# Two more split units per batch, paced indexed stores and moved small copies in a Fourier-mixing and maxout kernel

## The chip, the cores and the metric

The kernel runs on one core of one Trainium2 chip. The core has a matrix engine (TensorE, PE in the profile; its weight loads are PEld), a vector engine (VectorE, DVE), a scalar engine (ScalarE, ACT), a general engine (GpSimd, POOL) and a queue engine for transfers (SyncE, SP). Each engine works through its own instructions strictly in the order in which they were written; between engines, semaphores order the work. SBUF is the on-chip memory of 128 partitions, PSUM the accumulator memory into which PE writes, in banks of 512 float32 values for each partition. The metric is device time in microseconds (us) for one execution.

## The reference

```python
def _attn_ref(x):                      # x: (8, 3072, 256)
    X = np.fft.fft(x, axis=1)
    X = np.fft.fft(X, axis=2)
    return X.real.astype(np.float32)

def _moe_ref(x, w1, w2, w3, w_out):    # x: (24576, 256); w: (256, 768); w_out: (768, 256)
    h = np.maximum(np.maximum(x @ w1, x @ w2), x @ w3)
    return (h @ w_out).astype(np.float32)
```

The output of the first goes into the second as 24576 rows of 256. Inputs and output are float32.

## The kernel before

The Fourier transform over the 256 features is linear, so its cosine and sine matrices are multiplied into the weights once (`product`, `g_all`). The transform over the 3072 positions is done for each of the 8 batches in two steps (class `Mix`): `s` multiplies the input by a small table, `y` and `z` send the result through DRAM to change its layout (batch 0 uses one DVE transpose instead, `t`), and `k` multiplies it by cosine and sine tables into `tE` and `tO`, the parts of a frequency that are even and odd. A frequency and its mirror (3072 minus it) differ in the sign of the odd part alone. So 1536 frequencies are computed, as 3 blocks of 512, and each gives two output rows: "plus" and "minus", or mirror, rows.

The maximum of three products is taken as the maximum of zero and two differences, w2-w1 and w3-w1; the w1 part is added back by a matrix `gw`, which is w1 times the output weights. For one block of 512 frequencies the 768 hidden values come in 6 chunks of 128. One chunk of one block is a **unit**: 18 units a batch, 144 in all, numbered `g`, with `u` the number in its batch. A unit makes `hp` and `hm`, the hidden values of the plus and minus rows. There are two ways:

- A **plain** unit (`unit_plus`, `unit_minus`, `unit_out`) has six PE products of 512 columns: two into each of two banks for plus (L485, L486), then one into each that takes twice the odd part off (L492). ACT applies relu to one bank (L498) and DVE takes the maximum with the other (L499), once for plus, once for minus.
- A **split** unit forms the third difference ahead, in `third`: PE makes the even part e (L841) and the odd part d (L843); ACT copies d times -0.5 into `odd` (L845), DVE adds to e a term of the row that d lacks, the broadcast `vb` times a column of `wcol`, into `even` (L846), and POOL forms even+odd and even-odd (L850 twice). The unit then needs PE for the second difference alone (L860, L861, and L492 for minus), and one DVE operation for each maximum (L862, L874). That is five PE products. `third` is issued two units ahead.

`is_split` decides: from unit 7 on every odd unit; of the even ones, in batches 1 to 7, those in `EXTRA` (0, 4, 8), in batch 7 those in `EXTRA_LAST` (0, 4, 8, 14). When a plain unit follows a split one, the minus part of the old unit is done before the new one begins, otherwise after.

While a block's units run, PE also works off the second layer of the block before, ten steps a unit (`l2_some`, `l2_block`: L565, L572, L549); DVE adds the linear part and moves the results to one of three row buffers (L577). The last block of all goes through `l2_last`. Plus rows are stored by SP (`stores_plus`). Minus rows lie in reversed order, so POOL stores them with indirect DMA (L653): `rows_m` holds a row number for each partition, `stores_minus` lists the stores, and `scatter` takes them from a waiting list, one at u = 8, 10 and 12 and two at u = 14. Each is followed by a tiny memset.

A table `plan` says what else is issued at the end of which unit: the next batch's steps (`ahead`), loads of x for the batch after (`fetch`, a cast DMA from POOL's queue, in two halves of positions times two directions, at units 9, 11, 18 and 19, that is 0 and 1 of the next batch), and the mirrored half of x, copied by ACT (L128, one eighth at each of units 5 to 12, and L137). `u` copies one column of x into `x0u` (POOL, L442 and L443). `v` broadcasts row 0 of tO through DRAM to `vb`.

Before unit 0 of batch 0 there is a head: x arrives in four pieces, DVE and ACT mirror them (L128, L132), PE runs `s` with warm-up products between, DVE computes three tiny columns (`sgn`, `dif`; L217), evicts one result (L403) and transposes (L429), and `k` for block 0 fills `tE` and `tO` (L463). In unit 5 of batch 0 `rows` computes the row numbers on POOL and `column` (L351) the columns of `wcol` with 24 products of one column.

PSUM pools: `ps_f`, three banks, for e, d, the linear part and the steps of `Mix`; `ps_l1`, two, for the second difference of odd units and one bank of plain units; `ps_w3`, one, for the second difference of even split units and the other bank of plain even ones; `ps_o`, two, for the second layer.

Of the kernel before, what the change touches and what calls it, by code (L numbers as in the profile page):

```python
# [27 lines left out]


FIRST_OF = (4, 8, 1)  # L30
EXTRA, EXTRA_LAST = (0, 4, 8), (0, 4, 8, 14)


def _parts(g):

    done = [(12 + i - 1, slice(128 * i + 96, 128 * i + 128)) for i in range(4)]
    for i in range(4 if g < 2 else 3):
        done.append((FIRST_OF[g] + i - 1, slice(128 * i, 128 * i + 96)))
    if g == 2:
        done += [(16, slice(384, 480, 2)), (15, slice(385, 480, 2))]  # L40
    return done
# [3 lines left out]
def kernel(  # L45
# [9 lines left out]
    nc = tc.nc  # L55

    B, S, D = x.shape
# [4 lines left out]
    NHALF = 1536  # L62
# [46 lines left out]
    rows_m = consts.tile([128, 5], INT32, tag="rows_m")  # L109
# [13 lines left out]
    def mirror(b, s0, s1):  # L123

        t = xt[b % 2]
        fn = (nc.vector.tensor_copy, (nc.gpsimd.tensor_copy, nc.vector.tensor_copy)[s0 >= 25],
              nc.scalar.copy)[min(b, 2)]
        fn(out=t[64:128, s0:s1, 1:128], in_=t[0:64, s0:s1, 255:128:-1])  # L128
        if b < 2:
            if b == 0 and s0 < 40:  # L130
                fn = nc.scalar.copy
            fn(out=t[64:128, s0:s1, 0], in_=t[0:64, s0:s1, 128])  # L132

    def mirror_first(b):
# [59 lines left out]
    zero = gen.tile([128, 512], BF16, tag="zero")  # L194
    nc.vector.memset(zero, 0.0)
    nc.vector.memset(x0u, 0.0)
    half_pi = gen.tile([128, 1], FP32, tag="half_pi")
    nc.vector.memset(half_pi, 0.5 * math.pi)
    nc.scalar.activation(out=half_pi, in_=half_pi, func=AX.Sin)
# [145 lines left out]
    def column():  # L345

        psc = ps_f.tile([128, 512], FP32, name="psc", tag="ps")
        for jc in range(NJC):
            for k, (table, wt) in enumerate(((md, w3_bf), (nmd, w1_bf))):
                for fc in range(2):  # L350
                    nc.tensor.matmul(psc[:, jc:jc + 1],  # L351
                                     wt[:, fc * DFF + jc * 128: fc * DFF + jc * 128 + 128],
                                     table[fc][:, 128:129],
                                     start=(k == 0 and fc == 0), stop=(k == 1 and fc == 1))
        nc.scalar.copy(out=wcol, in_=psc[:, 0:NJC])

    def prep_second():
# [25 lines left out]
    class Mix:  # L383
# [55 lines left out]

        def u(self):  # L440
            pair = x0u[:, 32:160].rearrange("p (h z s) -> p h z s", h=2, s=32)[:, :, 0, 0:24]
            nc.gpsimd.tensor_copy(pair, self.x[0:128, 0:48, 0].rearrange("p (s h) -> p h s", h=2))  # L442
            nc.gpsimd.tensor_copy(x0u[:, 56:57], self.x[0:128, 48, 0:1])  # L443

        def x0(self, out):
            psx = ps_f.tile([128, 512], FP32, name="psx", tag="ps")
# [71 lines left out]
    def stores_plus(b, blk, buf, s0=0, s1=4):  # L518

        mine, v = rows_of(b)  # L520
        r, n = FIRST_OF[blk], s1 if blk < 2 else min(s1, 3)
        if s0 < n:
            yield v[0:96, r + s0:r + n, :], buf[0:96, s0:n, :]
        yield v[32 * blk:32 * blk + 32, 12 + s0:12 + s1, :], buf[96:128, s0:s1, :]
        if n < s1:
            yield mine[16:NHALF + 1:16, :], buf[0:96, 3, :]

    def stores_minus(b, blk, buf):

# [119 lines left out]
    def scatter(n):  # L649

        for _ in range(min(n, len(waiting))):
            row, col, p0, p1, src = waiting.pop(0)
            stored(nc.gpsimd.indirect_dma_start(  # L653
                fours, bass.IndirectOffsetOnAxis(ap=rows_m[p0:p1, col:col + 1], axis=0),
                src, None, element_offset=256 * row), "scattered", ("scattered", "direct"))
            nc.gpsimd.memset(mark, 0.0)

# [26 lines left out]
    mirror(0, *FIRST[3])  # L684
    m.s(4, pool=ps_s)
    warm_up(2)
    scal(sgn, pidx, 0.0, ALU.is_equal)
    scal(sgn, sgn, 2.0, ALU.mult, -1.0, ALU.add)
    scal(dif, sgn, 1.0, ALU.subtract)
    m.s(5, pool=ps_s, evict=dve)  # L690
    nc.scalar.activation(out=md_all, in_=vm, func=AX.Sin, scale=float(2.0 * math.pi / 256.0),
                         bias=turn[:, 0:1])
    m.s(6, pool=ps_s)
    m.t()
# [31 lines left out]

    def rows():

        rows_f = gen.tile([128, 5], FP32, tag="rows_f")
        for (c, n, base, cm) in ((0, 2, 766, -8), (2, 1, 767, -8), (3, 1, 252, -8), (4, 1, 764, -4)):  # L730
            iota(rows_f[:, c:c + n], [[-1, n]], base=base, cm=cm)
        adj = gen.tile([128, 2], FP32, tag="adj")
# [23 lines left out]
    def at(b, unit, fn):  # L756
        plan.setdefault((b + unit // UNITS, unit % UNITS), []).append(fn)
# [23 lines left out]
    def fetch(b, k):  # L781
        half, h = divmod(k, 2)
        load_x(b, *HALVES[half], h)
# [96 lines left out]
    for g in range(B * UNITS):  # L880
# [69 lines left out]
```

## Time and profile before

| what | value |
|---|---|
| median of 3 runs | 392.28 us (392.26 to 392.38) |
| profiled execution | 391.42 us, of which the span from first to last instruction is 389.3 |
| granted TensorE clock | 0.998 |
| batch 0, units 0 to 17 | 20 to 69 us |
| batches 1 to 6 | 44.3 us each |
| sums on POOL, L850 | 182 operations, 1271 and 1269 ns each |
| relu on ACT, L498; odd on ACT, L845 | 106 of 600 ns; 91 of 598 ns |
| even on DVE, L846 | 91 of 737 ns |
| hp and hm of split units on DVE, L862 and L874 | 91 of 688 and 91 of 680 ns |
| hp and hm of plain units on DVE, L499 | 106 of 686 to 689 ns |
| indirect stores, L653 | 37 of 997 to 1000 ns |
| x loads issued by POOL, L121 | 36 of 652 ns |

The profile counts an engine as busy while one of its instructions runs. Instructions of one engine overlap in the table: a product on PE is written with its whole way through the array, and a DVE operation with its start-up, so the distance between two starts can be shorter than one duration. A line of the timeline has the start in us, the duration in us, engine, line, operation and tiles; in brackets behind it stands the idle time of the engine before it and what ended that. A line of the stretches has the stretch, its length and the busy time of each engine in it with the number of instructions, then the granted clock, the share of the DMA engines and GB/s.

### The profile page before, as it was taken

Reading aid. Unit: us, or ns where it says so; the run is one execution under the profiler, and the core shown is the slowest. Engines: PE = TensorE matmul, PEld = TensorE weight load, DVE = VectorE, ACT = ScalarE, POOL = GpSimd, SP = SyncE. Lnnn points to the kernel's source line nnn. Section 1 sums busy time; section 2 is a strip of 40 time slices with the busy share of each in tenths; the row PEclk is TensorE's granted clock in tenths of the full one; section 3 lists DMA queues with packets and bytes.
Section 4 is the critical chain, followed back from the end, with each engine's and each line's share of the span. In section 5 each row is a group of like instructions: output and inputs, shape, how many; then the busy total and the mean of one; then the engine's idle time right before and its main releaser. Section 6 shows DMA issues by size and latency. Waiting matters only on the chain.

```text
span 389.3 us, 8092 instructions
## 1 busy us (share of the span) xinstructions
PE 376.2 (97%) x2817; PEld 236.2 (61%) x2817; DVE 327.7 (84%) x552; ACT 248.4 (64%) x453; POOL 314.3 (81%) x363
## 2 busy tenths in 40 slices
PE   6699999999999999999999999999999999999985
PEld 2355566566665666566665666656665666666654
DVE  7788797799797988899797988989887997999972
ACT  6877789567856696567856687567866346434420
POOL 9983576879898898879898898879787887769881
PEclk9999999999999999999999999999999999999999
DMA  7999764585747666475938657575423544212226
GB/s 113 184 183 160 163 145 118 112 168 161 178 141 130 172 176 154 111 128 186 189 120 149 169 151 176 125 128 185 113 94 93 149 138 139 70 31 80 85 89 206
DMA packets 52263, 54.13 MB, mean 139 GB/s; under 512 B 26547, under 2 KB 45009, under 8 KB 51367
## 3 DMA queue, kind: packets, MB, share of 16 engines
q0 software_dynamic: 20272, 26.45, 34.4%
q1 hardware_dynamic: 31418, 26.58, 25.0%
q10 hardware_dynamic: 532, 0.59, 0.5%
q8 instruction: 22, 0.36, 0.3%
q14 instruction: 19, 0.16, 0.1%
HBM read 36.95 MB, written 30.81 MB: 174 GB/s over the span
## 4 chain that ended last, share of the span: by engine, by line
PE 87%; POOL 4%; DVE 4%; DMA 2%; ACT 1%; issue 1%; DVEq 0%; POOLq 0%
PE po L549 30%; PE pse L492 10%; PE pse L860 5%; PE pse L485 5%; PE pse L486 5%; PE d L843 5%; PE e L841 5%; PE pse L861 5%; PE po L572 5%; PE ps L461 3%; PE ps L396 3%; PE pl L565 2%; DMA xt<-in_x_dram 2%; POOL xt L121 1%; POOL plus L850 1%
## 5 line engine op out<-in xcount | busy, mean ns | idle before, releaser
L850 POOL TENSOR_TENSOR plus<-even,odd 128x512 bf16<-128x512 f32 x91 | 115.7, 1271 | 55.4 <-DVE even L846 44.1
L850 POOL TENSOR_TENSOR minus<-even,odd 128x512 bf16<-128x512 f32 x91 | 115.5, 1269 | 0.0
L845 ACT ACTIVATE odd<-d 128x512 f32<-128x512 f32 x91 | 54.4, 598 | 55.8 <-PE d L843 41.9
L862 DVE SCALAR_TENSOR_TENSOR hp<-pse,plus 128x512 bf16<-128x512 f32 x91 | 62.6, 688 | 32.2 <-PE pse L861 27.9
L549 PE MATMUL po<-wout_bf,hp 128*128 128x256 bf16 x576 | 86.1, 273 | 0.0
L498 ACT ACTIVATE stmp<-pse 128x512 bf16<-128x512 f32 x106 | 63.2, 600 | 24.2 <-PE pse L486 11.2
L549 PE MATMUL po<-wout_bf,hm 128*128 128x256 bf16 x576 | 78.6, 273 | 0.0
L549 PEld LDWEIGHTS <-hp 128*128 128x128 bf16 x576 | 56.3, 98 | 26.2
L492 PE MATMUL pse<-tO,gd_all 128*128 128x512 bf16 x197 | 66.1, 380 | 1.3 <-DVE hp L862 1.3
L846 DVE SCALAR_TENSOR_TENSOR even<-vb,wcol,e 128x512 f32<-128x512 bf16 x91 | 67.1, 737 | 0.0
L549 PEld LDWEIGHTS <-hm 128*128 128x128 bf16 x576 | 56.3, 98 | 16.4
L874 DVE SCALAR_TENSOR_TENSOR hm<-pse,minus 128x512 bf16<-128x512 f32 x91 | 61.9, 680 | 0.4
L499 DVE TENSOR_TENSOR hp<-pse,stmp 128x512 bf16<-128x512 f32 x53 | 36.4, 686 | 8.8 <-ACT stmp L498 4.2
L499 DVE TENSOR_TENSOR hm<-pse,stmp 128x512 bf16<-128x512 f32 x53 | 36.5, 689 | 6.7 <-ACT stmp L498 4.3
L485 PE MATMUL pse<-tE,g_all 128*128 128x512 bf16 x106 | 40.2, 379 | 0.8 <-DVE tE L463 0.4
L577 DVE TENSOR_TENSOR kq<-po,even 128x512 f32<-128x512 f32 x60 | 40.9, 682 | 0.0
L128 ACT COPY xt<-xt 64x762 bf16<-64x762 bf16 (+1 forms) x48 | 39.8, 838 | 1.0
L486 PE MATMUL pse<-tO,g_all 128*128 128x512 bf16 x106 | 40.2, 379 | 0.0
L572 PE MATMUL po<-gw,tO 128*128 128x512 bf16 x92 | 34.9, 379 | 0.0
L860 PE MATMUL pse<-tE,g_all 128*128 128x512 bf16 x91 | 34.6, 380 | 0.1
L653 POOL DMA_INDIRECT out_dram<-kq,rows_m x29 | 29.0, 1000 | 6.8 <-issue 5.7
L841 PE MATMUL e<-tE,g_all 128*128 128x512 bf16 x91 | 34.5, 379 | 0.0
(173 smaller groups left out, 511.7 us busy)
## 6 DMA issues: line engine op xcount, KB each, us to landing
xt<-in_x_dram POOLq DMA_DIRECT2D x14, 384.0 KB
db<-tb SPq DMA_DIRECT2D x21, 192.0 KB
out_dram<-obuf SPq DMA_DIRECT2D x8, 384.0 KB
out_dram<-kq SPq DMA_DIRECT2D x8, 384.0 KB
vb<-vd SPq DMA_DIRECT2D x23, 128.0 KB
xt<-in_x_dram POOLq DMA_DIRECT2D x7, 400.0 KB
xt<-in_x_dram POOLq DMA_DIRECT2D x7, 368.0 KB
out_dram<-kq SPq DMA_DIRECT2D x7, 288.0 KB
```

The source lines that it names most:

```text
L485: nc.tensor.matmul(pse[:, 0:n], g_all[:, jc, 2 * i, :], te, start=True, stop=False)
L486: nc.tensor.matmul(pse[:, 0:n], g_all[:, jc, 2 * i + 1, :], to, start=False, stop=True)
L492: nc.tensor.matmul(pse, gd_all[:, jc, i, :], to, start=False, stop=True, skip_group_check=True)
L498: nc.scalar.activation(out=stmp[:, 0:n], in_=pses[0][:, 0:n], func=AX.Relu)
L499: nc.vector.tensor_tensor(out=dst, in0=src3, in1=stmp[:, 0:n], op=ALU.max)
L549: nc.tensor.matmul(po, hcols(jc), wout_bf[:, jc * 256:(jc + 1) * 256], start=False, stop=(jc == NJC - 1), skip_group_check=True)
L572: nc.tensor.matmul(po, to[:, cp], gw[:, 256:768], start=True, stop=True)
L845: nc.scalar.activation(out=odd3, in_=d3, func=AX.Copy, scale=-0.5)
L846: nc.vector.scalar_tensor_tensor(out=even3, in0=vb, scalar=wcol[:, jc:jc + 1], in1=e3, op0=ALU.mult, op1=ALU.add)
L850: nc.gpsimd.tensor_tensor(out=dst, in0=even3, in1=odd3, op=op)
L862: nc.vector.scalar_tensor_tensor(out=dst, in0=pse2, scalar=0.0, in1=sums[g][0], op0=ALU.max, op1=ALU.max)
L874: nc.vector.scalar_tensor_tensor(out=dst, in0=pses[0], scalar=0.0, in1=sums.pop(g)[1], op0=ALU.max, op1=ALU.max)
```

## The change

Units 12 and 14 are split in batches 1 to 6 as well, and unit 12 in batch 7. The mirror rows of the third block go out in two indirect stores of all 128 partitions (rows of 768 and of 256 values) in place of three of 96, 32 and 95; row 1536 is then written by the mirror store in all batches but the last. A waiting store is issued at units 0, 4, 8 and 14, in the last batch at 16 too. x is loaded in two issues a batch, one direction at unit 13 and the other at unit 18 (unit 0 of the next batch), from the load for batch 3 on. ACT makes the `x0u` copies of batches 1 to 7. `column` reads the columns from row 0 of `g_all` with six products. In the head, the last piece's column copy goes from DVE to POOL, the three `sgn` operations stand after the transpose, and block 0's `tE` and `tO` leave PSUM in two halves each, one by DVE and one by ACT (`k_first`).

```diff
-EXTRA, EXTRA_LAST = (0, 4, 8), (0, 4, 8, 14)
+PACE = (0, 4, 8, 14)
+EXTRA, EXTRA_LAST = (0, 4, 8, 12, 14), (0, 4, 8, 12, 14)
...
-            if b == 0 and s0 < 40:
-                fn = nc.scalar.copy
+            if b == 0:
+                fn = nc.scalar.copy if s0 < 40 else nc.gpsimd.tensor_copy
             fn(out=t[64:128, s0:s1, 0], in_=t[0:64, s0:s1, 128])
...
+    one = consts.tile([1, 1], BF16, tag="one")
+    nc.vector.memset(one, 1.0)
...
         for jc in range(NJC):
-            for k, (table, wt) in enumerate(((md, w3_bf), (nmd, w1_bf))):
-                for fc in range(2):
-                    nc.tensor.matmul(psc[:, jc:jc + 1],
-                                     wt[:, fc * DFF + jc * 128: fc * DFF + jc * 128 + 128],
-                                     table[fc][:, 128:129],
-                                     start=(k == 0 and fc == 0), stop=(k == 1 and fc == 1))
+            nc.tensor.matmul(psc[:, jc:jc + 1], g_all[0:1, jc, 3, :], one, start=True, stop=True)
...
-            nc.gpsimd.tensor_copy(pair, self.x[0:128, 0:48, 0].rearrange("p (s h) -> p h s", h=2))
-            nc.gpsimd.tensor_copy(x0u[:, 56:57], self.x[0:128, 48, 0:1])
+            fn = nc.scalar.copy if self.b else nc.gpsimd.tensor_copy
+            fn(out=pair, in_=self.x[0:128, 0:48, 0].rearrange("p (s h) -> p h s", h=2))
+            fn(out=x0u[:, 56:57], in_=self.x[0:128, 48, 0:1])
...
-            yield mine[16:NHALF + 1:16, :], buf[0:96, 3, :]
+            m = 96 if b == B - 1 else 95
+            yield mine[16:16 * m + 1:16, :], buf[0:m, 3, :]
...
-            return [(b * S + 1, blk, 0, 128, flat[:, 1024:2048])]
-        return [(b * S + 1, 2, 0, 96, flat[0:96, 1280:2048]),
-                (b * S + 1, 3, 0, 32, flat[96:128, 1024:2048]),
-                (b * S, 4, 0, 95, flat[0:95, 1024:1280])]
+            return [(b * S + 1, blk, fours, flat[:, 1024:2048])]
+        return [(b * S, 2, out, flat[:, 1280:2048]), (b * S, 3, out, flat[:, 1024:1280])]
...
-    scal(sgn, pidx, 0.0, ALU.is_equal)
-    scal(sgn, sgn, 2.0, ALU.mult, -1.0, ALU.add)
-    scal(dif, sgn, 1.0, ALU.subtract)
     m.s(5, pool=ps_s, evict=dve)
...
+    def k_first(which):
+        for h in range(2):
+            ps2 = ps_s.tile([128, 512], FP32, name="ps2", tag="ps")
+            for (i, cols) in _parts(0):
+                at = cols.start - 256 * h
+                if 0 <= at < 256:
+                    nc.tensor.matmul(ps2[:, at:at + cols.stop - cols.start], m.col(i, which),
+                                     (te_tab, to_tab)[which][:, cols], start=True, stop=True)
+            (dve, nc.scalar.copy)[h](out=(m.tE, m.tO)[which][:, 256 * h:256 * h + 256],
+                                     in_=ps2[:, 0:256])
     m.s(6, pool=ps_s)
     m.t()
+    scal(sgn, pidx, 0.0, ALU.is_equal)
+    scal(sgn, sgn, 2.0, ALU.mult, -1.0, ALU.add)
+    scal(dif, sgn, 1.0, ALU.subtract)
...
-    m.k(0, 0, dve)
-    m.k(1, 0)
+    k_first(0)
+    k_first(1)
...
-        for (c, n, base, cm) in ((0, 2, 766, -8), (2, 1, 767, -8), (3, 1, 252, -8), (4, 1, 764, -4)):
+        for (c, n, base, cm) in ((0, 2, 766, -8), (2, 1, 3069, -32), (3, 1, 3056, -16)):
             iota(rows_f[:, c:c + n], [[-1, n]], base=base, cm=cm)
-        for (c, far) in ((0, 766.0), (1, 511.0)):
-            scal(adj[:, c:c + 1], pidx, 96.0, ALU.is_ge, far, ALU.mult, eng=nc.gpsimd)
-        nc.gpsimd.tensor_tensor(out=rows_f[:, 0:2], in0=rows_f[:, 0:2], in1=adj, op=ALU.add)
+        for (c, base, cm) in ((0, 766, 0), (1, 511, 0), (2, 1013, 0), (3, 1025, -16)):
+            iota(adj[:, c:c + 1], [[0, 1]], base=base, cm=cm)
+        scal(far, pidx, 96.0, ALU.is_ge, eng=pool)
+        scal(adj, adj, far, ALU.mult, eng=pool)
+        pool.tensor_tensor(out=rows_f, in0=rows_f, in1=adj, op=ALU.add)
...
-        for ch in range(4):
+        for h in range(2):
             if b > 2:
-                at(b - 3, (9 + (b == 3), 11, 18, 19)[ch], lambda b=b, ch=ch: fetch(b, ch))
+                at(b - 3, (13, 18)[h], lambda b=b, h=h: load_x(b, 0, NS, h))
...
-        scatter({8: 1, 10: 1, 12: 1, 14: 2}.get(u, 0))
+        if u in PACE or (b == B - 1 and u == 16):
+            scatter(1)
```

More of the change, by code (lines that the diff above doesn't have):

```diff
@@ L108 @@
     obuf = consts.tile([128, 2048], FP32, tag="obuf")
-    rows_m = consts.tile([128, 5], INT32, tag="rows_m")
+    rows_m = consts.tile([128, 4], INT32, tag="rows_m")
     mark = consts.tile([1, 1], FP32, tag="mark")
@@ L651, in scatter @@
         for _ in range(min(n, len(waiting))):
-            row, col, p0, p1, src = waiting.pop(0)
+            row, col, dst, src = waiting.pop(0)
             stored(nc.gpsimd.indirect_dma_start(
-                fours, bass.IndirectOffsetOnAxis(ap=rows_m[p0:p1, col:col + 1], axis=0),
+                dst, bass.IndirectOffsetOnAxis(ap=rows_m[:, col:col + 1], axis=0),
                 src, None, element_offset=256 * row), "scattered", ("scattered", "direct"))
@@ L686 @@
     warm_up(2)
+    m.s(5, pool=ps_s, evict=dve)
+    nc.scalar.activation(out=md_all, in_=vm, func=AX.Sin, scale=float(2.0 * math.pi / 256.0),
+                         bias=turn[:, 0:1])
+    def k_first(which):
[8 more added lines that the diff above has]
+                                     in_=ps2[:, 0:256])
+    m.s(6, pool=ps_s)
+    m.t()
     scal(sgn, pidx, 0.0, ALU.is_equal)
@@ L689 @@
     scal(dif, sgn, 1.0, ALU.subtract)
[L690 to L694, printed above, removed]
     warm_up(2)
@@ L727, in rows @@
     def rows():
-        rows_f = gen.tile([128, 5], FP32, tag="rows_f")
-        for (c, n, base, cm) in ((0, 2, 766, -8), (2, 1, 767, -8), (3, 1, 252, -8), (4, 1, 764, -4)):
-            iota(rows_f[:, c:c + n], [[-1, n]], base=base, cm=cm)
-        adj = gen.tile([128, 2], FP32, tag="adj")
-        for (c, far) in ((0, 766.0), (1, 511.0)):
-            scal(adj[:, c:c + 1], pidx, 96.0, ALU.is_ge, far, ALU.mult, eng=nc.gpsimd)
-        nc.gpsimd.tensor_tensor(out=rows_f[:, 0:2], in0=rows_f[:, 0:2], in1=adj, op=ALU.add)
+        pool = nc.gpsimd
+        rows_f = gen.tile([128, 4], FP32, tag="rows_f")
+        adj = gen.tile([128, 4], FP32, tag="adj")
+        far = gen.tile([128, 1], FP32, tag="far")
+        for (c, n, base, cm) in ((0, 2, 766, -8), (2, 1, 3069, -32), (3, 1, 3056, -16)):
+            iota(rows_f[:, c:c + n], [[-1, n]], base=base, cm=cm)
+        for (c, base, cm) in ((0, 766, 0), (1, 511, 0), (2, 1013, 0), (3, 1025, -16)):
[3 more added lines that the diff above has]
+        pool.tensor_tensor(out=rows_f, in0=rows_f, in1=adj, op=ALU.add)
         nc.gpsimd.tensor_copy(rows_m, rows_f)
```

## The prediction

> **What bounds the kernel now.** I read the page's busy shares and the chain of waits first, then busy time by stretches, then the timeline of TensorE (PE), and last the timelines of the other engines against it.
>
> ```profile
> PE 376.2 (97%) x2817; PEld 236.2 (61%) x2817; DVE 327.7 (84%) x552; ACT 248.4 (64%) x453; POOL 314.3 (81%) x363
> PEclk9999999999999999999999999999999999999999
> ...
> PE 87%; POOL 4%; DVE 4%; DMA 2%; ACT 1%; issue 1%; DVEq 0%; POOLq 0%
> ```
>
> Three engines are above 80%, but 87% of the chain that ended last is PE, and the granted clock is full all along. Busy time by stretches, one full batch (18 units) and then the last ones:
>
> ```profile
> core 0: us, PE busy (x) PEld busy (x) DVE busy (x) ACT busy (x) POOL busy (x), PEclk, DMA share, GB/s
> ...
> 160.70:205.00 44.30, 44.30 (x333) 27.99 (x332) 38.35 (x61) 30.93 (x56) 38.20 (x41) 1.00 0.65 153
> ...
> 370.00:389.30 19.30, 13.37 (x104) 9.75 (x102) 9.74 (x16) 2.27 (x4) 9.48 (x14) 0.95 0.47 149
> ```
>
> In a batch PE has no idle time at all; DVE has 5.95 us of it and POOL 6.10 us. Busy PE could still be PE waiting inside a pipeline, so the spacing of its starts matters. A split unit on PE, by time:
>
> ```profile
> 203.39 0.38 PE L860 MATMUL pse<-tE,g_all 128*128 128x512 bf16 x1
> 203.60 0.38 PE L861 MATMUL pse<-tO,g_all 128*128 128x512 bf16 x1
> 203.82 0.38 PE L492 MATMUL pse<-tO,gd_all 128*128 128x512 bf16 x1
> 204.04 0.38 PE L841 MATMUL e<-tE,g_all 128*128 128x512 bf16 x1
> 204.25 0.38 PE L843 MATMUL d<-tO,gd_all 128*128 128x512 bf16 x1
> ```
>
> Each 512-column product is written as 0.38 us, but they start 0.215 us apart, with the next work right behind. So a product taken away is worth 0.215 us and no more, and PE sets the pace of the batches. Only the end differs:
>
> ```profile
> 370.07 1.28 POOL L850 TENSOR_TENSOR plus<-even,odd 128x512 bf16<-128x512 f32 x1
> ...
> 371.39 0.69 DVE L862 SCALAR_TENSOR_TENSOR hp<-pse,plus 128x512 bf16<-128x512 f32 x1 [1.85 <-PE po L549]
> ...
> 372.14 0.38 PE L492 MATMUL pse<-tO,gd_all 128*128 128x512 bf16 x1 [0.76 <-DVE hp L862]
> ...
> 375.23 1.28 POOL L850 TENSOR_TENSOR plus<-even,odd 128x512 bf16<-128x512 f32 x1
> ...
> 376.54 0.69 DVE L862 SCALAR_TENSOR_TENSOR hp<-pse,plus 128x512 bf16<-128x512 f32 x1 [0.81 <-POOL plus L850]
> ...
> 377.28 0.38 PE L492 MATMUL pse<-tO,gd_all 128*128 128x512 bf16 x1 [0.59 <-DVE hp L862]
> ```
>
> In the last batch, where PE has no next batch to prepare, POOL is late: hp of units 15 and 17 starts within 0.05 us of the end of POOL's sum (370.07+1.28, 375.23+1.28), and PE stands 0.76 and 0.59 us. By PE's own starts these are 0.92 and 0.75 us beyond the normal step.
>
> **Units 12 and 14.** A plain unit is six such products (L485 and L486 twice each, L492 twice; 106 = 2x53 of L485 says 53 plain units), a split one five. Units 12 and 14 of batches 1 to 6 and unit 12 of batch 7 (14 was split there) make 13: 13x0.215 = 2.8 us off PE, 0.43 us a batch. ACT loses one of two evictions of 0.60 us per unit. What has to carry it:
>
> DVE gains one L846 per unit; back to back it costs 0.66 us (353.56 to 354.22), 1.3 us a batch out of 5.95 idle. That is cover, if it lies in the right place. At units 10 to 12 DVE has almost none, so I followed the waits there, in the batch from 157.4. The new products of unit 12 come at 182.27; its L846 follows hp of unit 10 at 183.54, and what is behind moves by 0.65: hp of 11 to 184.8, hm of 10 to 185.4-186.1. PE's first product of unit 12 now needs that hm at once, since it writes the single bank that unit 10 used (before, two products into another buffer came first), at 186.0+0.43-0.215 = 186.2. So it fits with 0.1 us to spare. The next: L846 of unit 13 ends 186.7 (PE needs it 187.3), odd of 14 ends 188.15 on ACT (needed 188.4), L846 of 14 ends 189.2 (needed 189.5). Unit 12's 0.96 us of DVE idle time at 188.94 then takes the queue up. I take no new stall; if each of these margins is missed by 0.1 us, 0.2 to 0.4 us a batch come back, 1.2 to 2.4 in all.
>
> POOL gains 2x(1.271+1.269) = 5.08 us a batch. It loses an indirect store with its memset (1.000+0.088), the x0u copies (0.261+0.188), and two of four load issues (0.56, 0.80, 0.56, 0.77 in the timeline): between nothing, if an issue costs by its size, and 1.33. So 38.20+5.08-1.09-0.45 = 41.7 down to 40.4 us, of 43.9. The order: sums of 11 end 184.3 as now; 12 to 186.8; 13 to 189.4; 14 to 191.85; 15 to 194.35 (2.47 us each, back to back, stores no longer between); load issue and one store to 196.5; 17 to 199.1. Each plus is ready before its hp: 15 at 193.1 for 194.1, 17 at 197.8 for 199.5. At the next unit 0 a store and a load delay the sums of unit 3 by 0.7 us, which wait 2.5 us for hp today. So POOL's work stays hidden, at 0.
>
> Here I weigh a rule against the row. The row is PE at 0.215 us a product without gaps. The Trainium skill (Perfetto Trace Analysis, Identifying the Most-Contended Engine) says that matmul busy share is a poor measure, that weight loads' share is to be used, and that the engine with the highest occupancy is the one to relieve. That is 61% for PE and 84% for DVE here, and by it the change loads the wrong engines; the sum would be that of the second rival below.
>
> **Stores and loads.** The third block's mirror rows go out in two stores of 128 partitions instead of three of 96, 32 and 95; the indirect rows last 0.9 to 1.15 us for each of these, so I take 1.0. They leave at units 0, 4, 8, 14 instead of 8, 10, 12, 14, 14; each buffer is rewritten at least 4 units (10 us) later. Loads of x go in two issues, units 13 and 18, instead of four. Software DMA moved 26.45 MB in 34.4% of the span, 134 us: 197 GB/s; so 752 KB take about 4 us, plus about 2 before the first packet. In the batch from 201.7 the second one is issued near 206 and lands by 212 to 214; the first mirror copy on ACT (171.98 in the batch before, so 216.3) needs it. That wait has 2 us of cover. Cost 0.
>
> **Small copies.** The x0u copies on ACT cost some 0.6 us (L137's 64x49 copy is 0.41, L451's one column 0.17) and fall into 2.1 us of ACT idle time before 171.36. Cost 0; without that cover, odd of unit 7 is 0.6 late.
>
> **Batch 0.** The column of weights takes 6 products instead of 24 (24 take 0.60 us by their starts of 0.025): 0.45 less, bound below by 0; I take 0.35. Row numbers cost POOL three more small operations (0.12 to 0.23 each), beside 8.3 us of idle time. The head: the three sgn operations go behind the transpose, tE and tO leave in halves on DVE and ACT. The eviction at 14.51 waited for PE anyway, so the transpose hardly moves; sgn then holds the first half tE till 19.6, done 20.05 instead of 20.30, and tO 20.41 instead of 20.54. Gain 0.1, between -0.3 (a loss, if POOL's column copy waits behind its DMA issues) and 0.3.
>
> **Last batch.** Between units 8 and 15 POOL loses three stores (8, 10, 12, 14, 14 become 8 and 14) of about 1.2 us with their waits and gains one pair of 2.47. Its sums of 14 and 15 follow the flip copies: 15 starts 369.6 instead of 370.07, so PE's first stall shrinks by some 0.25. One store instead of two stands before 17's sums: 373.5 instead of 375.23, and PE's second stall goes, 0.75. That is 1.0, bounds 0 and 1.4 (DVE has no idle time from 353 to 364); I take 0.75.
>
> **Sum:** 2.8 + 0.75 + 0.35 + 0.1 = 4.0 us. The profiled execution took 391.42 us, 389.3 of it the span; 387.4 is forecast for it. The median of the runs is 392.28, 0.86 higher, so 388.3 there.
>
> **The rivals.** First, the small margins at units 10 to 14 are missed: 1.2 to 2.4 us come back, and the last batch gives nothing: 390.2 to 391.4. For: 0.1 us is less than I can place. Against: DVE starts 0.60 us apart with great regularity.
>
> Second, the side that is slower: POOL becomes the pace of the batch. 28 sums at 1.235 are 34.6, four stores with memset and wait 1.4 each 5.6, loads 2.7: 42.9 us. If every plus also waits 0.15 us after its L846, as nearly all do now, 45.0 against 44.3 before: 0.7x6 = 4.2 longer, 396.5. It decides once the queue stands above 43.9, 1.0 more than without waits. Against: where POOL is late today (366.49, 370.07) that wait is gone. The rule of the Trainium skill named above points the same way; with DVE as the pace it would be 13x0.66 = 8.6 longer, 401.
>
> Third, the longer load at unit 13 (issue 194.4) delays the vb broadcast that DVE needs at 198.39 for the next batch. It is issued at 192.65 now, some 0.8 later then; the round trip before it took 3.2. If it were served wholly behind the load, 4 us, it would come 2.3 late, in five batches: 11.5 - 4 = 7.5 longer, 400; from 1.7 us of delay on it decides. Fourth, gains fall short everywhere and it comes out within 0.2% (0.8 us), which is what a measurement here cannot tell from no change.
>
> **How the numbers follow.** Forecast, 387.3 to 389.8: 0.64 (gains of 2.8+1.4+0.45+0.3 at the low end, 2.8+0+0-0.3 at the high one). First rival: 0.17. Still lower, to 386.8: 0.02. Fourth: 0.06. Second: 0.07. Third: 0.04. Faster is 0.64+0.17+0.02 = 0.83, within 0.06, slower 0.11. The range takes the forecast and the first rival: 386.8 to 391.4.
>
> **What would show it.** Right: 104 of L846's kind, a batch of 43.9 us with PE without gaps, POOL near 41 us in it, hp of the last unit not waiting for plus. Wrong: PE waiting for hm, for even's eviction or for plus around units 12 to 15; DVE waiting for vb at unit 16; ACT waiting for x at unit 5.

## The result and the profile after

| | before | after |
|---|---|---|
| median of the runs beside each other | 392.28 us (5 runs, 391.87 to 393.08) | 388.26 us (5 runs, 387.35 to 388.61) |
| profiled execution, and its span | 391.42, 389.3 | 388.26, 386.5 |
| batch 0, from its first unit | 49.07 us | 48.78 us |
| batch 1 | 41.90 us | 42.44 us |
| batches 2 to 6, each | 44.29 (the last 44.18) us | 43.85 (the last 43.75) us |
| from the last mark to PE's last start | 51.79 us | 50.33 us |
| from PE's last start to the end | 4.88 us | 5.15 us |

The ratio of after to before is 0.9892, with an interval of 0.9875 to 0.9909: 4.0 us less, clear of the noise, and the median is the one that was forecast. (Every ratio below, too, is to the kernel before, in runs taken beside it.) The ends of batches are marked by an ACT copy that comes once in each (`t_mid`, a result of the steps `ahead`); a first such mark stands inside batch 0, at 33.73 us before and 33.97 after. The marks around batch 3, before and then after, are 44.29 and 43.85 us apart:

```profile
155.61 0.17 ACT L478 CAST t_mid<-ps 128x2 bf16<-128x2 f32 x1
199.90 0.17 ACT L478 CAST t_mid<-ps 128x2 bf16<-128x2 f32 x1
...
155.69 0.17 ACT L477 CAST t_mid<-ps 128x2 bf16<-128x2 f32 x1
199.54 0.17 ACT L477 CAST t_mid<-ps 128x2 bf16<-128x2 f32 x1
```

The two profiled executions lie only 3.16 us apart (2.85 in their spans), since the one of before was 0.86 us below the median of its kernel.

The shares and the chain of the kernel after, from its page:

```profile
PE 369.5 (96%) x2737; PEld 234.8 (61%) x2786; DVE 335.7 (87%) x566; ACT 242.7 (63%) x455; POOL 331.7 (86%) x355
PEclk9999999999999999999999999999999999999999
...
PE 81%; POOL 9%; DVE 4%; issue 3%; ACT 2%; DVEq 0%; POOLq 0%
```

DVE and POOL are busier than before (87% and 86%, from 84% and 81%), the time is shorter, and PE still holds 81% of the chain. Only 2737 products are recorded beside 2786 weight loads (before, 2817 of each), so PE's share is understated. Busy time by stretches, in the columns of the prediction: one full batch, then the last 19.3 us.

```profile
155.00:198.85 43.85, 43.43 (x329) 27.80 (x332) 39.28 (x63) 29.98 (x55) 40.53 (x38) 1.00 0.66 157
367.10:386.40 19.30, 14.19 (x109) 10.32 (x107) 10.39 (x18) 2.27 (x4) 9.88 (x13) 1.00 0.44 144
```

A batch takes 43.85 us where it took 44.29. PE's 43.43 is short of that because records are missing (329 products here); in the kernel with loads in four issues below, whose trace has all of them, PE is busy 43.85 of 43.85 us. POOL's 40.53 lies between the 40.4 and 41.7 that the prediction worked out, and DVE has 39.28. POOL has 3.3 us left in a batch. The tightest margin that the prediction named, at unit 12, in the timeline of the same batch:

```profile
185.48 0.68 DVE L498 TENSOR_TENSOR hm<-pse,stmp 128x512 bf16<-128x512 f32 x1
...
186.31 0.38 PE L875 MATMUL pse<-tE,g_all 128*128 128x512 bf16 x1
```

hm of unit 10 ends at 186.16, and PE's first product of unit 12, which writes the bank that this frees, starts at 186.31, with no wait in brackets. That is the order and nearly the place of the forecast (186.1 and 186.2). In the last batch POOL's sum, hp, and the PE product that waited before (L491 is the line that was L492, L865 was L850, L877 was L862, L875 was L860, L498 on DVE was L499):

```profile
367.69 1.28 POOL L865 TENSOR_TENSOR plus<-even,odd 128x512 bf16<-128x512 f32 x1
...
369.01 0.69 DVE L877 SCALAR_TENSOR_TENSOR hp<-pse,plus 128x512 bf16<-128x512 f32 x1 [1.16 <-POOL plus L865]
...
369.75 0.38 PE L491 MATMUL pse<-tO,gd_all 128*128 128x512 bf16 x1 [0.25 <-DVE hp L877]
...
374.15 0.38 PE L491 MATMUL pse<-tO,gd_all 128*128 128x512 bf16 x1
```

At unit 15 hp still starts as POOL's sum ends (367.69+1.28), and PE stands (waits) 0.41 us by its starts instead of 0.92. At unit 17 nothing is waited for, instead of 0.75. And a wait that was not there before, in batch 1:

```profile
72.82 1.01 POOL L122 DMA_DIRECT2D xt<-in_x_dram  x1
...
84.82 0.82 ACT L129 COPY xt<-xt 64x762 bf16<-64x762 bf16 x1 [1.32 <-DMA xt<-in_x_dram]
...
88.74 0.69 DVE L498 TENSOR_TENSOR hm<-pse,stmp 128x512 bf16<-128x512 f32 x1 [0.49 <-ACT stmp L497]
...
89.48 0.38 PE L875 MATMUL pse<-tE,g_all 128*128 128x512 bf16 x1 [0.54 <-DVE hm L498]
```

The load issued at 72.82 reaches ACT's mirror copy 12.0 us later, and ACT stands 1.32 us. The relus that follow on ACT (L497) come late for it, and so do hm and PE's product at 89.48, 0.70 us by its starts. At 98.61 PE stands another 0.19 for hm, at unit 12. So batch 1 is 0.54 us longer than before, though it has two products less. In the later batches ACT does not wait for x.

The difference of the spans, stretch by stretch (a plus is longer than before): up to the first mark +0.24; rest of batch 0, with the column, -0.26; batch 1 +0.54; batches 2 to 6 -2.18; from the last mark to PE's last start -1.46; last stores +0.27. The sum is -2.85.

### The profile page after: what moved, and what is told of

Same layout as the page of the kernel before. It is cut to its first block, busy times and chain, and to the rows that moved or that the text cites. A ratio compares the mean times of both kernels' runs of the same rounds, so it can differ in the third digit from the quotient of the medians.

```text
span 386.5 us, 7957 instructions
## 1 busy us (share of the span) xinstructions
PE 369.5 (96%) x2737; PEld 234.8 (61%) x2786; DVE 335.7 (87%) x566; ACT 242.7 (63%) x455; POOL 331.7 (86%) x355
## 4 chain that ended last, share of the span: by engine, by line
PE 81%; POOL 9%; DVE 4%; issue 3%; ACT 2%; DVEq 0%; POOLq 0%
PE po L547 29%; PE pse L491 9%; PE pse L876 5%; PE e L856 5%; PE d L858 5%; PE pse L875 5%; PE po L570 4%; PE pse L485 4%; PE pse L484 3%; PE ps L460 3%; POOL plus L865 3%; PE ps L394 3%; PE pl L563 2%; POOL minus L865 2%; POOL xt L122 1%
## 5 line engine op out<-in xcount | busy, mean ns | idle before, releaser
L865 POOL TENSOR_TENSOR plus<-even,odd 128x512 bf16<-128x512 f32 x104 | 132.0, 1269 | 38.5 <-DVE even L861 31.1
L865 POOL TENSOR_TENSOR minus<-even,odd 128x512 bf16<-128x512 f32 x104 | 132.1, 1270 | 0.0
L860 ACT ACTIVATE odd<-d 128x512 f32<-128x512 f32 x104 | 62.1, 597 | 63.8 <-PE d L858 50.3
L877 DVE SCALAR_TENSOR_TENSOR hp<-pse,plus 128x512 bf16<-128x512 f32 x104 | 71.4, 687 | 26.0 <-PE pse L876 21.5
L861 DVE SCALAR_TENSOR_TENSOR even<-vb,wcol,e 128x512 f32<-128x512 bf16 x104 | 76.6, 737 | 0.0
L491 PE MATMUL pse<-tO,gd_all 128*128 128x512 bf16 x183 | 63.2, 380 | 0.8 <-DVE hp L877 0.2
L497 ACT ACTIVATE stmp<-pse 128x512 bf16<-128x512 f32 x80 | 47.5, 599 | 19.0 <-PE pse L491 8.8
L129 ACT COPY xt<-xt 64x762 bf16<-64x762 bf16 (+1 forms) x48 | 39.8, 838 | 2.3 <-DMA xt<-in_x_dram 1.3
L858 PE MATMUL d<-tO,gd_all 128*128 128x512 bf16 x104 | 39.4, 379 | 0.0
L498 DVE TENSOR_TENSOR hp<-pse,stmp 128x512 bf16<-128x512 f32 x40 | 27.5, 687 | 6.7 <-ACT stmp L497 3.6
L875 PE MATMUL pse<-tE,g_all 128*128 128x512 bf16 x84 | 31.9, 380 | 0.7 <-DVE hm L498 0.5
L567 ACT COPY even<-pl 128x512 f32<-128x512 f32 x46 | 26.8, 583 | 8.3 <-DVE kq L575 7.8
L498 DVE TENSOR_TENSOR hm<-pse,stmp 128x512 bf16<-128x512 f32 x40 | 27.5, 687 | 4.2 <-ACT stmp L497 3.0
```

The source lines that it names most:

```text
L491: nc.tensor.matmul(pse, gd_all[:, jc, i, :], to, start=False, stop=True, skip_group_check=True)
L498: nc.vector.tensor_tensor(out=dst, in0=src3, in1=stmp[:, 0:n], op=ALU.max)
L858: nc.tensor.matmul(d3, gd_all[:, jc, 1, :], to, start=True, stop=True)
L860: nc.scalar.activation(out=odd3, in_=d3, func=AX.Copy, scale=-0.5)
L861: nc.vector.scalar_tensor_tensor(out=even3, in0=vb, scalar=wcol[:, jc:jc + 1], in1=e3, op0=ALU.mult, op1=ALU.add)
L865: nc.gpsimd.tensor_tensor(out=dst, in0=even3, in1=odd3, op=op)
```

## The experiments

Theory: PE sets the pace of the batches, a split unit takes 0.215 us off it, and POOL can carry two more only because it loses a store and the others are spread over the batch. Rivals: POOL's order does not matter and the units alone are the gain; the gain is the clearing of POOL at the end; the fewer loads and copies are what makes room. "After" and "before" below are the two kernels; each edit is against the one named.

### The units alone (edit of before)

```diff
-EXTRA, EXTRA_LAST = (0, 4, 8), (0, 4, 8, 14)
+EXTRA, EXTRA_LAST = (0, 4, 8, 12, 14), (0, 4, 8, 12, 14)
```

> The kernel before with units 12 and 14 split in batches 1 to 6 and unit 12 in batch 7, and nothing else of the change. Theory (POOL's work is hidden only because stores and loads leave the stretch from unit 8 to 15): POOL must do five sums of two, three stores of about 1.2 us and two load issues there; walked through as in the prediction, the sums of unit 15 end 198.4 instead of 194.35 in the batch from 157.4, hp of 15 waits some 3 us for plus, so each of 6 batches loses about 2 to 3 us net of the 0.43 saved: 400 to 412. Rival (POOL's 6 us of idle time in a batch hold the 5.08 wherever they lie): 392.3 - 2.8 = 389.5.

401.95 us (401.62 to 403.0, 4 runs), ratio 1.0261 (1.0244 to 1.0278): 10 us slower than the kernel before. Batches with loads take 46.15 us, those without 44.86 and 44.53. A batch by stretches, and then its unit 15 in the timeline:

```profile
157.40:203.50 46.10, 43.88 (x324) 27.84 (x329) 38.96 (x63) 29.91 (x53) 42.90 (x45) 1.00 0.65 147
```

```profile
199.04 0.90 POOL L653 DMA_INDIRECT out_dram<-kq,rows_m  x1 [0.18 <-issue]
...
199.99 1.28 POOL L850 TENSOR_TENSOR plus<-even,odd 128x512 bf16<-128x512 f32 x1
...
201.30 0.69 DVE L862 SCALAR_TENSOR_TENSOR hp<-pse,plus 128x512 bf16<-128x512 f32 x1 [2.34 <-POOL plus L850]
...
202.04 0.38 PE L492 MATMUL pse<-tO,gd_all 128*128 128x512 bf16 x1 [1.41 <-DVE hp L862]
```

This is the chain of the second rival of the prediction: a store stands on POOL ahead of the sum, hp waits 2.34 us for it, and PE waits 1.41 for hp. POOL is busy 42.90 of 46.10: it is not full over the batch, it is full from unit 10 to unit 15, where the stores stood. Splitting units with the stores in their old places is therefore a loss.

### Everything but the units (edit of after)

```diff
-EXTRA, EXTRA_LAST = (0, 4, 8, 12, 14), (0, 4, 8, 12, 14)
+EXTRA, EXTRA_LAST = (0, 4, 8), (0, 4, 8, 14)
```

> The changed kernel with the old sets of split units (0, 4, 8, and 14 in the last batch): all of the change but units 12 and 14. Theory (the stores' new places clear POOL in the last batch, about 1.5 us; column 0.27 gained; head 0.25, a late load in batch 1 and the tail lost): 1 us faster than the kernel before, 390.6 to 391.8. Rival (the gain of the last batch comes from unit 12 being split): no faster than the kernel before, 392.0 to 393.

390.47 us (389.51 to 392.11, 10 runs), ratio 0.9961 (0.9946 to 0.9976), a little below the expected time. Batches take 44.28, as before. So the units are worth 390.47 - 388.26 = 2.2 us in the changed kernel (2.00 by PE's last start) and -10 in the one before. The end is better without them: 49.89 us from the last mark to PE's last start, against 51.79 before and 50.33 after. Unit 15 of the last batch:

```profile
371.01 0.69 DVE L877 SCALAR_TENSOR_TENSOR hp<-pse,plus 128x512 bf16<-128x512 f32 x1 [0.68 <-POOL plus L865]
...
372.00 0.38 PE L491 MATMUL pse<-tO,gd_all 128*128 128x512 bf16 x1
```

hp still waits for POOL, but PE does not wait for hp. The stores, in new places and two instead of three for the third block, take away both stalls of the last batch, which is 1.90 us shorter in this stretch, and unit 12 split in the last batch brings 0.44 back. Batch 1 takes 42.71, with 1.34 us of waiting on ACT: the late load has nothing to do with the units.

### The units with paced stores, but three of them (edit of before)

```diff
-EXTRA, EXTRA_LAST = (0, 4, 8), (0, 4, 8, 14)
+EXTRA, EXTRA_LAST = (0, 4, 8, 12, 14), (0, 4, 8, 12, 14)
...
-        scatter({8: 1, 10: 1, 12: 1, 14: 2}.get(u, 0))
+        if u in (0, 4, 8, 11, 14) or (b == B - 1 and u == 16):
+            scatter(1)
```

> The kernel before with units 12 and 14 split and only the places of its five stores a batch changed: units 0, 4, 8, 11 and 14, and 16 in the last batch; three stores for the third block, loads and copies as before. Theory (PE needs hp of 15 about 1.5 us after it could start; with the loads in the old places hp started 0.92 us late at no cost, and one store of 1.2 us more, at unit 11, goes beyond): 0.3 to 0.5 us of stall in the batches with loads, 44.1 to 44.4, and 43.85 in 5 and 6; 389.5 to 391. Rival (taking two of the five stores out of units 8 to 15 is enough): 43.85 everywhere, 388.5.

391.14 us (390.58 to 391.62, 9 runs), ratio 0.9972 (0.996 to 0.9984), a little above the expected time. With the same operations on POOL as the first experiment, but in another order, the kernel takes 10.8 us less. Yet batches with loads take 44.32 us, no less than before. The same place in the timeline:

```profile
194.33 1.27 POOL L850 TENSOR_TENSOR plus<-even,odd 128x512 bf16<-128x512 f32 x1
...
195.64 0.69 DVE L862 SCALAR_TENSOR_TENSOR hp<-pse,plus 128x512 bf16<-128x512 f32 x1 [1.16 <-POOL plus L850]
...
196.38 0.38 PE L492 MATMUL pse<-tO,gd_all 128*128 128x512 bf16 x1 [0.15 <-DVE hp L862]
```

PE starts 0.33 us late here in each batch, and POOL is busy 43.02 of 44.32 us. So the order of the stores takes the loss away, but not yet the last stall. The next kernel has the same loads, the store at unit 11 gone and the small copies on ACT, with POOL at 41.71 us of a batch, and no such stall; the run with the copies back on POOL, further down, shows no stall in batches 2 to 6 either, so it is the store that counts, as far as these runs separate the three. Whether a fifth store at another unit, outside 8 to 15, would have done as well was not tried: that POOL's work has to shrink, and not only to leave this stretch, is not shown.

### Loads in four issues as before (edit of after)

```diff
-        for h in range(2):
+        for ch in range(4):
             if b > 2:
-                at(b - 3, (13, 18)[h], lambda b=b, h=h: load_x(b, 0, NS, h))
+                at(b - 3, (9 + (b == 3), 11, 18, 19)[ch], lambda b=b, ch=ch: fetch(b, ch))
```

> The changed kernel, with the loads of x in four issues a batch at units 9 (10 for batch 3), 11, 18 and 19 as before. Theory (two issues of 0.56 and 0.77 us among the sums of units 11 to 15 make plus of 15 end 0.3 to 0.5 us after PE could use it; in the run with the units alone, batches with these loads took 46.15 and one without 44.86): batches 2 to 4 at 44.1 to 44.5 instead of 43.85, batches 5 and 6 unchanged; batch 1 loses the late load (0.8 better) but has the same wait: 388.5 to 389.5. Rival (POOL has room for them): batches stay at 43.85, 0.8 us faster than the changed kernel by batch 1.

387.66 us (387.28 to 387.82, 4 runs), ratio 0.9886 (0.9869 to 0.9902). Here the theory missed and its rival held: batches take 43.85 us, as after, with POOL at 41.71. Its wait did come, but without a cost:

```profile
193.78 0.69 DVE L877 SCALAR_TENSOR_TENSOR hp<-pse,plus 128x512 bf16<-128x512 f32 x1 [0.92 <-POOL plus L865]
...
195.34 0.39 PE L491 MATMUL pse<-tO,gd_all 128*128 128x512 bf16 x1
```

hp of unit 15 waits 0.92 us for POOL and ends at 194.47; PE wants it at 195.34. The prediction asked that plus be ready before hp *could* start (194.1 in its batch); what counts is when PE *needs* hp, 0.9 us after it ended even here. The merged loads bought nothing in the batches. Batch 1 takes 41.65 us with them in four issues, and ACT does not wait there.

### Batch 3's load alone in four issues, two of them early (edit of after)

```diff
-            if b > 2:
+            if b > 3:
                 at(b - 3, (13, 18)[h], lambda b=b, h=h: load_x(b, 0, NS, h))
+        for ch in range(4):
+            if b == 3:
+                at(b - 3, (10, 11, 18, 19)[ch], lambda b=b, ch=ch: fetch(b, ch))
```

> The changed kernel, with the load of batch 3 alone in four issues at units 10, 11, 18 and 19 as before. Theory (in batch 1 the load issued at unit 0 lands late, ACT waits 1.32 us for it at unit 5 and PE stands 0.70 and 0.19 us for it later): 0.7 to 1.0 us faster than the changed kernel, ACT without that wait, batch 1 at 41.5 us. Rival (batch 1 lengthens because units 12 and 14 are too much for DVE or POOL there): same as the changed kernel within 0.3.

388.20 us (387.8 to 389.01, 5 runs), ratio 0.9907 (0.9894 to 0.9921). Batch 1 is 0.80 us shorter (41.64), as the theory had it; the 0.19 at unit 12 stays (0.18 here), so it does not come from the load. The load's first issues on POOL, and the mirror copy on ACT, which has no wait in brackets any more:

```profile
72.78 0.59 POOL L122 DMA_DIRECT2D xt<-in_x_dram  x1
...
83.35 0.82 ACT L129 COPY xt<-xt 64x762 bf16<-64x762 bf16 x1
```

PE's last start is 0.64 us earlier (380.68), but the profiled execution ended later, as 6.17 us passed from there to the end (4.6 to 5.4 in all other kernels). The time cannot be told from that of after, so the 0.7 to 1.0 us are met in the trace and not by the times. Over all versions of the changed kernel, ACT waits for this load in each of the six with two issues (0.53 to 1.88 us; batch 1 takes 41.60 to 43.11) and in none of the four versions of it with four (41.46 to 41.65).

### One more split unit, 10 (edit of after)

```diff
-EXTRA, EXTRA_LAST = (0, 4, 8, 12, 14), (0, 4, 8, 12, 14)
+EXTRA, EXTRA_LAST = (0, 4, 8, 10, 12, 14), (0, 4, 8, 12, 14)
```

> The changed kernel, with unit 10 split too in batches 1 to 6, so that units 7 to 15 are all split. Theory (POOL then is the pace of that stretch: nine pairs of 2.47 us and a store from 172.9 on in the batch from 157.4 end plus of 15 at 195.2, 1.3 us after PE could use it): batches 44.6 to 45.3 instead of 43.85, PE waiting for hp behind plus: 392 to 397. Rival (PE sets the pace everywhere, each split unit is worth 0.215): 387.0, batches 43.64.

392.03 us (390.98 to 393.01, 10 runs), ratio 1.000 (0.9988 to 1.0012): the whole gain is gone. Batches take 44.48. A batch by stretches, then its unit 12:

```profile
157.60:202.08 44.48, 43.78 (x329) 27.81 (x328) 39.61 (x64) 29.59 (x56) 42.83 (x41) 1.00 0.63 153
```

```profile
187.49 0.69 DVE L877 SCALAR_TENSOR_TENSOR hp<-pse,plus 128x512 bf16<-128x512 f32 x1 [0.27 <-POOL plus L865]
188.10 0.68 DVE L889 SCALAR_TENSOR_TENSOR hm<-pse,minus 128x512 bf16<-128x512 f32 x1
...
188.83 0.38 PE L875 MATMUL pse<-tE,g_all 128*128 128x512 bf16 x1 [0.70 <-DVE hm L889]
```

One unit takes 0.215 us off PE and puts 2.5 on POOL, whose sums now come late. hp of unit 11 waits for plus, hm of unit 10 stands behind it on DVE, and PE's first product of unit 12 waits for the bank that hm frees: 0.84 us by its starts. The theory had the size nearly (44.48 for 44.6 to 45.3) but looked for the stall at unit 15; it sits at the 0.1 us margin that the prediction had named.

### The last batch's stores (edit of after)

```diff
-        if u in PACE or (b == B - 1 and u == 16):
+        if u in ((0, 4, 8, 12, 14) if b == B - 1 else PACE):
```

> The changed kernel, with the stores of the last batch at units 0, 4, 8, 12 and 14 instead of 0, 4, 8, 14 and 16. Theory (a store ahead of the sums of 15 and one ahead of those of 17 delay hp of both): the last batch, from the copy to t_mid at 330.99 to the last product, takes 51.3 to 52.2 us instead of 50.33. Rival (the last batch gains by unit 12 and not by the stores' places): 50.3.

388.98 us in a single run. The last stretch takes 51.59 us against 50.33, as the theory had it, and by PE's starts the stall at unit 15 is 1.68 instead of 0.41:

```profile
371.03 0.38 PE L491 MATMUL pse<-tO,gd_all 128*128 128x512 bf16 x1 [1.52 <-DVE hp L877]
```

Two stores issued two units earlier, in one batch, cost 1.26 us: the end hangs on where they stand in POOL's queue.

### The head (edit of after)

```diff
-                fn = nc.scalar.copy if s0 < 40 else nc.gpsimd.tensor_copy
+                fn = nc.scalar.copy if s0 < 40 else nc.vector.tensor_copy
```

> The changed kernel, with the last piece's column copy in the head on DVE again. Theory (that copy stands on POOL behind the row-ramp operations, and the fifth step of the head starts 0.25 us later for it): 0.25 us faster than the changed kernel, first unit at 20.37 instead of 20.62. Rival (the three operations moved behind the transpose, or the halves of tE and tO, cost it): same as the changed kernel.

388.26 us (387.64 to 389.33, 5 runs), ratio 0.9909 (0.9893 to 0.9925). No gain, so the theory missed: here DVE's copy of x (L129) took 0.88 us and the column's copy, on DVE too, 0.48, and the step behind them started at 14.47, against 14.31 after.

### Small copies back on POOL (edit of after)

```diff
-            fn = nc.scalar.copy if self.b else nc.gpsimd.tensor_copy
+            fn = nc.gpsimd.tensor_copy
```

> The changed kernel, with the x0u copies on POOL again in all batches. Theory (0.45 us of POOL's idle time at unit 3 takes them): batches 2 to 6 at 43.85 as in the changed kernel. Rival (POOL's queue needs that time before the sums of 5 to 7): batches 43.9 to 44.3.

388.56 us in a single run. Batches 2 to 6 take 43.85 (the last 43.75), the end 50.33: the copies are worth nothing on either engine, as forecast. This trace shows more of the head, which is the same program as after. DVE's copy of x, POOL's row numbers, and the column copy that stands behind them:

```profile
12.93 0.66 DVE L129 COPY xt<-xt 64x1143 bf16<-64x1143 bf16 x1 [0.85 <-DMA xt<-in_x_dram]
13.22 1.04 POOL L145 IOTA kq<- 128x288 f32 x4
14.33 0.22 POOL L133 COPY xt<-xt 64x9 bf16<-64x9 bf16 x1
```

DVE has ended at 13.59, and POOL takes the column up at 14.33, behind its four row-number operations. x came early here, and 0.74 us of that was lost. In the kernel after POOL took it up at 14.04, 0.03 us behind the copy. (Later in this head, from 15.0 to 21.7 us, the granted clock was 0.75, against 1.00 after, and the first unit starts 1.06 us later than after.)

### Two versions put together

The first (edit of after) is the kernel with batch 3's load in four issues, with unit 12 plain and 14 split in the last batch. The second (edit of after) has all loads in four issues, the same last batch, and the head of before (column copy on DVE, `sgn` ahead of the transpose, `tE` and `tO` whole). The first lines below stand in both, the last in the second alone; the lines for the loads and for the rest of the head are as shown above:

```diff
-EXTRA, EXTRA_LAST = (0, 4, 8, 12, 14), (0, 4, 8, 12, 14)
+EXTRA, EXTRA_LAST = (0, 4, 8, 12, 14), (0, 4, 8, 14)
...
-    k_first(0)
-    k_first(1)
+    m.k(0, 0, dve)
+    m.k(1, 0)
```

> The changed kernel, with the load of batch 3 in four issues as in the third run and unit 12 plain in the last batch. Theory (the late load costs 0.8 in batch 1; in the last batch, where POOL is late, unit 12's pair costs more than the product it saves: 50.33 us with it, 49.89 in the run of the rest alone): 1.2 us faster than the changed kernel, up to 0.5 either way for the end of the last stores: 387.0. Rival (the stores' places alone cleared POOL, and a split unit 12 is worth 0.2 there as elsewhere): the last batch 50.5, 387.7.

> The changed kernel with the loads of x in four issues at the old units, unit 12 plain in the last batch, and the whole head as before (column copy on DVE, the three sgn operations ahead of the eviction, tE and tO leaving in one piece each). Theory (the late load costs 0.8, unit 12 of the last batch 0.44, and the head's edits nothing but jitter: from the end of the transpose to the first unit it was 1.29 us before and 1.30 after): 386.7 to 387.4; transpose end to first unit 1.29. Rival (the halves of tE and tO do gain, hidden by jitter): 1.5 us from transpose end to first unit, 387.5.

387.38 us (387.16 to 388.38, 4 runs), ratio 0.9889 (0.987 to 0.9907), and 387.54 us (386.52 to 388.12, 5 runs), ratio 0.9875 (0.9856 to 0.9895). Both were forecast slightly lower (387.0, and 386.7 to 387.4). In both, the last stretch takes 49.89 us with neither stall, as expected, and batch 1 41.65 and 41.46. PE's last start is at 380.38 and 380.32, 0.94 and 1.00 earlier than after; the medians are 0.9 and 0.7 lower, but the intervals overlap with that of after, so this gain is seen in the traces and not established by the times. From the end of the transpose to the first unit 1.29 us pass in the old head of the second version and 1.30 in the new head of after.

## Why the prediction was right, and where it was not

The time, the direction and the main mechanism were right: 4.0 us forecast and 4.0 measured by the medians. For the profiled execution 387.4 was forecast and 388.26 came: from profile to profile the gain is 3.16 us, and 2.85 of span, where 4.0 was summed. The medians hide this, since the 0.86 us that the profile of before lay below its median has no counterpart after. Single executions of one kernel differ by about 1 us, so that the median was met this closely is in part luck; the terms tell more.

**Units 12 and 14: 0.43 a batch.** Right in batches 2 to 6, 0.44 each. The walk through POOL's queue (sums of 12 done at 186.8, 13 at 189.4, 14 at 191.85, 15 at 194.35) was met to 0.16 us: the trace of after has 186.96, 189.42, 191.88 and 194.31 for the starts of what follows. "So it fits with 0.1 us to spare" was nearly exact: hm ended 0.15 us ahead in the batch shown, and in single batches of several versions, batch 1 of after among them, PE stood 0.1 to 0.2 there.

**The last batch, two errors that oppose each other.** The stalls were put at 0.75, computed as 1.0, with 1.4 as the upper bound; the change without the units made the stretch 1.90 shorter. Unit 12 was to give 0.215 there; splitting it cost 0.44, in a stretch in which PE waits for hp of unit 15 and hp for POOL. Together 1.46, where 0.97 was forecast. (DVE was said to have no idle time from 353 to 364 there; the timeline has 0.21 us, before 356.30.)

**"That wait has 2 us of cover. Cost 0."** Wrong in one batch. The load was priced by the mean rate of all software transfers, at 6 to 8 us from issue to landing; in batch 1 it took 11.9, and ACT's copy came 12.0 after the issue. This is the largest missing piece: batch 1 became 0.54 longer instead of 0.43 shorter, and with the early load it is 0.80 shorter again. ACT waiting for x at unit 5 was one of the prediction's own signs of being wrong. In batches 2 to 5 the same load took 7.6 to 8.8 us, and the cover held. Its lead was not at fault: from the issue until ACT wanted x 10.7 us passed in batch 1 and 10.4 in the others. Why this one load takes so long was not tried.

**"Each plus is ready before its hp."** True, but a stricter demand than was needed. With the loads as before hp did wait, and PE did not. So the two load issues saved on POOL, counted in the prediction as part of what makes room, were not needed for it.

**Column 0.35, head 0.1, small copies 0.** The stretch with the column became 0.26 shorter. The head gave no 0.1: the halves of tE and tO gave nothing (1.29 and 1.30 us from transpose to first unit), because the first unit starts when the last half of tO has left, at 20.57, and not when tE has, at 20.23. From the start of DVE's copy of x to the step that needs both copies 0.69 to 0.78 us passed in the four kernels with the old head, and 0.79 to 1.67 in the eight with POOL's copy. But in the one run that puts the copy alone back on DVE 1.34 passed, so it is not shown that POOL's copy is what costs. Where it does wait, as in the run with the small copies, it is the kind of loss that the lower bound of -0.3 had named ("if POOL's column copy waits behind its DMA issues"), only behind the row numbers. As x itself arrives up to 1.3 us earlier or later, no time shows it.

**The rivals.** Of the first, only batch 1 and single batches show the margin missed. The second, POOL as the pace, did not come true for this change, but it is real on both sides of it: without the stores' new order (10 us slower) and with one unit more (the gain gone). Its point was put at a queue above 43.9 us; the kernel with unit 10 stalls at 42.83 busy, and the one with three paced stores at 43.02, as waits come on top. The third is not seen in batches 2 to 6, where the gain is whole; the fourth is not, with 1.1% gained. As to the rule of the Trainium skill (Perfetto Trace Analysis, Identifying the Most-Contended Engine) that was weighed there: with DVE and POOL, the highest shares, each loaded further, the batch became 0.44 us shorter. So the trace goes against the rule, as the prediction applied it, for this step. That page names two measures for TensorE, MFU (the products done, against the peak) beside the weight loads' share; the prediction used the second alone, and what the trace speaks against is that 61% as a measure of PE. MFU was not worked out. For the next unit the rule agrees: there POOL, at 42.83 of 44.48, sets the time.

## What to carry to other kernels

An engine with idle time in a batch may be full just where it counts: the same operations on POOL, some 43 us of a batch, cost 10 us in one order and nothing in another, so walk the queue by time around the tightest consumer rather than adding up its busy time. Ask of each wait when the bounding engine *needs* the result, not when the next engine could start. And a change that fits everywhere in the steady batches still has to be checked in the first, where here one load took 11.9 us instead of 7.6 to 8.8, and in the last, where PE waited for POOL before and after.

## What the runs showed of the hardware

An indirect store cost POOL about 1.0 us (0.85 to 1.20 over all traces, mean 1.00 in each) whether it wrote 32, 96 or 128 partitions, so two large ones cost less than three small ones. The issue of a load cost POOL 0.55 to 0.62 and 0.76 to 0.86 us in turn with four issues, and 0.55 to 0.61 and 1.00 to 1.02 with two, though the second of the two is the smaller (752 KB, in rows taken in reverse, against 784): it does not go by size.

DVE's copy of 64x1143 in the head takes 0.48 to 0.50 us in four traces and up to 0.88 in others. The longest began 0.3 us after the first of POOL's four row-number operations (13.13, these from 12.84 to 13.98), two of the shortest 0.7 us after it (13.56, from 12.83) or at their end (14.21, to 14.23); the traces between do not order so cleanly. The Trainium skill (SBUF — State Buffer, SBUF: two separate sides) says that DVE and GpSimd share a pair of ports that, for some kinds of DVE operations, one of the two holds for a whole instruction while the other is blocked. The extra 0.4 us is about one of these operations, 0.29 to 0.46 us as written in that trace, which would agree with it. But the column's copy behind it took 0.48 us too, against 0.16 in the kernel before, although it began at 13.94, as these operations ended. No run here shows whether the copies are of such a kind, and none took the operations away, so the cause stays open.
